# The last product of a three-stage attention/FFN kernel, written as seven quarter products

## The chip, the cores and the metric

One core of one Trainium2 chip runs the whole program. The metric is device time in microseconds (us) of one execution. Three runs of the kernel before took 1508.46, 1511.51 and 1515.61 us, a median of 1511.51. The engines are TensorE (PE in the rows; PEld is its weight load), VectorE (DVE), ScalarE (ACT), GpSimd (POOL) and SyncE (SP), whose queue issues the DMAs.

## What is computed

All inputs are float32 for the kernel except the six weight matrices, which arrive as float64 and are turned into float32 on the chip.

```python
kv = einsum('bhsd,bhse->bhde', k, v); out = einsum('bhsd,bhde->bhse', q, kv)   # 8 batches, 8 heads, 576 x 64
x = out / sqrt(mean(out*out, -1) + 1e-6) * g_norm                              # then 4608 tokens x 512
x = max(x @ w1, x @ w2, x @ w3) @ moe_w_out                                    # 512 -> 768 -> 512
g = s * relu(x @ w_in)**2 + b                                                  # 512 -> 2048
result = g @ w_out                                                             # 2048 -> 512
```

## The kernel before, in words

Tokens are kept in nine blocks of 512 columns with the features on the partitions: block b has the first 512 tokens of batch b, the ninth the last 64 tokens of all eight batches. Every float32 operand of a matmul is split into a high and a low part (`split`: a ScalarE copy, then a subtraction on VectorE or GpSimd), and each product is three matmuls (high x high, high x low, low x high).

Three stages follow one another on TensorE.

*Stage 1* does attention, norm and the first FFN, block by block, and writes the result to `x1d` in device memory. Beside it, w_in and w_out are read as float64 in 32 pieces (`p2_src`, `conv_load`), converted (`conv_unpack`, `conv_sum`) and stored to `wd`.

*Stage 2* is the w_in product by Strassen's scheme (Winograd's form). A set `q` of inputs is two blocks side by side; there are four wide sets (2 x 512 columns) and one narrow (2 x 256). `right` makes the seven inputs of a set, `left` the seven factors of each of four weight groups. For each set and group, `product` runs seven quarter products of 12 matmuls into PSUM tiles a, b and c, two each, some of them adding onto a tile that holds an earlier one. `combine` copies products 0, 1 and 2 out (ScalarE, the "cs" tiles), adds them to products 3, 4 and 5 (VectorE), squares (VectorE; GpSimd for product 6) and scales (`s*g+b`, ScalarE). `keep` stores the four quarters of the result in `gd`. That makes 20 groups of 7 x 12 matmuls.

*Stage 3* is the w_out product, tile by tile in the plain way: w_out is the moving operand (512 columns), a 128-token slice of g the stationary one. `g_load` reads g back, `g_split` splits it into one of six slots (tags h0 to h5), `gemm4` adds 16 x 3 matmuls for each of four token slices of a block into `acc`, `last_out` copies that out (ScalarE and VectorE in turn) and `store` writes 128 whole rows of the result, 2 KB each; for the ninth block two stores of 64 rows.

What sets the order: each step is put at a position of a plan by `at(pos, ...)` and sorted. On TensorE and SP the instructions stand in that order; on the other engines a scheduler orders them by a simulated time. A position in stages 2 and 3 is 12 matmuls; `T4` is where stage 3 starts. The steps that the change touches are planned in lines 705 to 731.

## Time and profile before

| | |
|---|---|
| median of three runs | 1511.51 us |
| the profiled execution, its own time | 1511.72 us |
| its span, first to last instruction | 1509.9 us |
| TensorE busy | 1437.8 us, 95% |
| VectorE, ScalarE, GpSimd busy | 744.6, 668.3, 415.5 us |
| DMA, mean over the span | 119 GB/s |

Busy time of an instruction runs from its start to its end; matmuls, and operations of VectorE and ScalarE, start before the one ahead has ended, so a rate is read from starts. "idle before <-X" in a row is the time for which the engine stood still ahead of it and the instruction whose end released it. A row of the profile that begins with L612 belongs to line 612 of the kernel.

### The profile page before, as it was taken

The page shows a single profiled execution, that of the slowest core. Times are in us where ns is not written, and L with a number is a line of the kernel's source. Part 1 is how long each engine was busy: PE and PEld are TensorE (multiplying, and loading weights), DVE is VectorE, ACT ScalarE, POOL GpSimd, SP SyncE. Part 2 cuts the span into 40 slices and gives each one's busy share as a digit, 9 for nine tenths or more (in the row PEclk, how much of TensorE's full clock was granted, in tenths as well). Part 3 has the DMA queues.
Part 4 walks back from the last instruction along what each step waited for, and adds up shares of the span by engine and source line. Part 5 has one row for each costly group of instructions (what it writes and reads, how often), then busy time and mean ns, then how long its engine had stood idle before and what let it go on. Part 6 is the DMA issues. An engine that isn't in the chain of part 4 may idle for free. (4 is left out here: it accounts for less than half of the span.)

```text
span 1509.9 us, 18507 instructions
## 1 busy us (share of the span) xinstructions
PE 1437.8 (95%) x6868; PEld 1173.1 (78%) x6868; DVE 744.6 (49%) x1129; ACT 668.3 (44%) x1153; POOL 415.5 (28%) x301
## 2 busy tenths in 40 slices
PE   4777899999999999999999999999999999999998
...
GB/s 206 198 190 87 63 73 103 90 125 102 126 87 140 87 139 22 112 8 112 77 105 158 136 112 175 95 163 129 192 251 137 77 86 120 139 140 140 139 84 28
DMA packets 173579, 179.48 MB, mean 119 GB/s; under 512 B 91440, under 2 KB 126256, under 8 KB 171824
## 3 DMA queue, kind: packets, MB, share of 16 engines
...
q14 instruction: 37, 0.30, 0.1%
...
## 5 line engine op out<-in xcount | busy, mean ns | idle before, releaser
L94 PE MATMUL g<-xh,w_w 128*128 128x512 f32 x648 | 258.3, 401 | 4.6 <-ACT xh L90 4.6
L95 PE MATMUL g<-xl,w_w 128*128 128x512 f32 x648 | 257.4, 397 | 0.0
L96 PE MATMUL g<-xh,w_w 128*128 128x512 f32 x648 | 256.9, 397 | 0.0
L680 PE MATMUL acc<-w_z,g 128*128 128x512 f32 x576 | 224.1, 389 | 0.0
L681 PE MATMUL acc<-w_z,g 128*128 128x512 f32 x576 | 224.1, 389 | 0.0
L682 PE MATMUL acc<-w_z,g 128*128 128x512 f32 x576 | 224.1, 389 | 0.0
L612 PE MATMUL ps_a<-x_q,w_q 128*128 128x512 f32 (+1 forms) x960 | 209.6, 369 | 7.2 <-ACT cs L621 5.6
L90 ACT ACTIVATE g<-gr 128x512 fp32r<-128x512 f32 x144 | 90.9, 631 | 267.7 <-PE acc L682 250.7
L91 DVE TENSOR_TENSOR g<-gr,g 128x512 fp32r<-128x512 f32 x108 | 75.6, 700 | 268.7 <-ACT g L90 267.4
L612 PEld LDWEIGHTS ps_a<-x_q,w_q 128*128 128x128 f32 x960 | 167.3, 188 | 41.2 <-ACT cs L621 8.4
L632 ACT ACTIVATE r<-r,sb_b,sb_s 128x512 f32<-128x512 f32 (+1 forms) x160 | 118.6, 766 | 82.1 <-DVE r L628 36.7
L94 PEld LDWEIGHTS g<-xh,w_w 128*128 128x128 f32 x648 | 123.4, 191 | 32.3 <-ACT xh L90 6.2
L95 PEld LDWEIGHTS g<-xl,w_w 128*128 128x128 f32 x648 | 124.2, 192 | 27.1 <-POOL tr_ctr L162 0.5
L96 PEld LDWEIGHTS g<-xh,w_w 128*128 128x128 f32 x648 | 123.9, 191 | 27.5 <-issue 0.5
L523 POOL TENSOR_TENSOR r<-r 128x512 f32<-128x512 f32 (+1 forms) x40 | 54.9, 1383 | 311.1 <-ACT r L630 309.8
L91 POOL TENSOR_TENSOR g<-gr,g 128x512 fp32r<-128x512 f32 x36 | 47.1, 1307 | 335.7 <-ACT g L90 335.7
L681 PEld LDWEIGHTS acc<-w_z,g 128*128 128x128 f32 x576 | 108.1, 188 | 22.5
L682 PEld LDWEIGHTS acc<-w_z,g 128*128 128x128 f32 x576 | 108.1, 188 | 22.4
L680 PEld LDWEIGHTS acc<-w_z,g 128*128 128x128 f32 x576 | 108.1, 188 | 22.3
L162 POOL TENSOR_TENSOR tr_ctr<-tr_ctr 128x512 int32<-128x512 int32 x42 | 55.5, 1320 | 197.9 <-ACT tr_ctr L155 181.4
L612 PE MATMUL ps_b<-x_q,w_q 128*128 128x512 f32 (+1 forms) x480 | 105.8, 369 | 0.8 <-ACT cs L621 0.7
L361 DVE TENSOR_TENSOR h<-g,h 128x512 f32<-128x512 f32 x108 | 74.0, 685 | 53.1 <-PE g L96 51.9
...
## 6 DMA issues: line engine op xcount, KB each, us to landing
gd<-r SPq DMA_DIRECT2D x128, 256.0 KB, 2.0
gr<-gd SPq DMA_DIRECT2D x64, 512.0 KB, 6.5
raw_craw<-in_moe_w_out_dram SPq DMA_DIRECT2D x20, 512.0 KB, 3.8
...
raw_craw<-in_moe_w_in_dram SPq DMA_DIRECT2D x16, 512.0 KB, 4.2
...
```

Of the source, the lines that this page charges most:

```text
L90: act(out=hi, in_=src, func=AF.Copy)
L91: eng.tensor_tensor(out=lo, in0=src, in1=hi.bitcast(F32), op=ALU.subtract)
L94: nc.tensor.matmul(ps, lhsT=w[:, 0, sl], rhs=xh, start=first, stop=False)
L95: nc.tensor.matmul(ps, lhsT=w[:, 0, sl], rhs=xl, start=False, stop=False)
L96: nc.tensor.matmul(ps, lhsT=w[:, 1, sl], rhs=xh, start=False, stop=last)
L162: nc.gpsimd.tensor_tensor(out=t, in0=t, in1=r, op=ALU.add)
L361: nc.vector.tensor_tensor(out=st["h", m], in0=ps, in1=st["h", m], op=ALU.max)
L612: nc.tensor.matmul(ps, lhsT=w[:, a, c], rhs=x[:, b_, :n], start=new and k == 0 and e == 0, stop=k == HK - 1 and e == 2, skip_group_check=True)
L632: act(out=h, in_=h, func=AF.Identity, scale=sb_s, bias=sb_b)
L680: mm(acc, lhsT=h[:, 0, sl], rhs=w[:, 0], start=(k == 0), stop=False)
L681: mm(acc, lhsT=h[:, 0, sl], rhs=w[:, 1], start=False, stop=False)
L682: mm(acc, lhsT=h[:, 1, sl], rhs=w[:, 0], start=False, stop=(k == M2 - 1))
```

## The change

Stage 3 now uses the seven quarter products too. The result is made feature-major. The 2048 inputs of w_out are cut in two parts, so each set has two *halves* H (10 in all, H even: first part, H odd: second), each with 7 products of 4 inputs x 2 output tiles x 3 matmuls, added up over the two parts in `xh`/`xl` tiles. The moving operand is now g (512 or 256 columns), the stationary one a factor of w_out.

Around that: `combine` keeps its result in the "cs" tile (a ring of 10, was 6), squares product 6 on ScalarE, gives products 3 and 6 the opposite sign, and adds two pairs on GpSimd, so that `gd` holds five quarters, with one sum of inputs made ready. `left` makes 28 factors of w_out during the last set of stage 2 (before: 16 splits), three of seven negated. w_out is loaded as float64 in four DMAs a piece, with columns in another order. After each odd half, `put` turns the result in squares of 32 x 32 on VectorE and stores it with four DMAs from 32 partitions each (512 B runs); for the narrow set, eight DMAs. The tiles of `put` are four: two tagged "t" and two "st".

```diff
+    neg = base.tile([P, 2], F32, name="neg")
-    gd = [dram.tile([P, 4, M2 // 2, N], F32, name=f"gd{q}") for q in range(B // 2 + 1)]
+    gd = [dram.tile([P, 5, M2 // 2, N], F32, name=f"gd{q}") for q in range(B // 2 + 1)]
...
     def p2_src(n):
-        n -= M2
-        return [(0, P, w2o[n * P:(n + 1) * P, :])]
+        r0 = i * DF2 // 2 + 2 * m * P
+        return [((2 * kk + b) * P, None,
+                 w2o[r0 + kk * P:r0 + (kk + 1) * P, :].rearrange("p (a b r) -> p b a r", a=4, b=4)[:, 2 * j + b])
+                for kk in range(2) for b in range(2)]
...
     def combine(G, q, g, i):
             if i < 3:
-                s_ = st["cs", i, m] = p2["pool"].tile([P, N], F32, tag="s", bufs=6, name=f"cs_{G}_{i}_{m}")
+                s_ = st["cs", i, m] = p2["pool"].tile([P, N], F32, tag="s", bufs=10, name=f"cs_{G}_{i}_{m}")[:, :n]
...
             if i < 6:
-                tt(nc.vector, h, ps, add, st["cs", {3: 2, 4: 1, 5: 0}[i], m][:, :n])
+                h = st["cs", 5 - i, m]
+                tt(nc.vector, h, ps, add, h)
+                stt(out=h, in0=h, scalar=0.0, in1=h, op0=ALU.max, op1=ALU.mult)
             else:
+                h = stage2(f"r_{G}_{m}")[:, :n]
                 act(out=h, in_=ps, func=AF.Relu)
-                tt(nc.gpsimd, h, h, ALU.mult, h)
-            act(out=h, in_=h, func=AF.Identity, scale=sb_s, bias=sb_b)
+                act(out=h, in_=h, func=AF.Square)
+            less = i in (3, 6)
+            act(out=h, in_=h, func=AF.Identity, scale=neg[:, 0:1] if less else sb_s, bias=neg[:, 1:2] if less else sb_b)
+            if i == 6:
+                d = st["r", 7, m] = stage2(f"d_{G}_{m}")[:, :n]
+                tt(nc.gpsimd, d, st["r", 4, m], add, h)
+                tt(nc.gpsimd, h, st["r", 5, m], add, h)
...
+    def z_right(H, i, k_):
+        n, z = width(H // 2), lambda i_: p2["z", i_, k_]
+        if i in (2, 3):
+            tt(nc.vector, z(1), z(1), add, z(0 if i == 2 else 5))
+        f = z(1 if 0 < i < 4 else i)
+        o = 28 * H + 4 * i + k_
+        x = hs["z", i, k_] = slot(HS[o % M1], f"zx_{o}")
+        split(x[:, 0, :n], x[:, 1, :n], f, nc.gpsimd if o % 6 == 5 else nc.vector)
+
+    def z_product(H, i, k_):
+        n, new = width(H // 2), i in (0, 1, 5)
+        kk = 4 * (H % 2) + k_
+        w, x = wt["q", 4 + kk // 2, i], hs["z", i, k_]
+        for m in range(2):
...
+            for e, (a, b_) in enumerate(((0, 0), (0, 1), (1, 0))):
+                nc.tensor.matmul(ps, lhsT=w[:, a, c], rhs=x[:, b_, :n], start=new and k_ == 0 and e == 0,
+                                 stop=k_ == 3 and e == 2, skip_group_check=True)
+
+    def z_combine(H, i):
...
+            if i < 3:
+                s_ = st["cs", i, m] = p2["pool"].tile([P, N], F32, tag="s", bufs=10, name=f"zc_{H}_{i}_{m}")[:, :n]
+                act(out=s_, in_=ps, func=AF.Copy)
+                if more:
+                    tt(nc.gpsimd, s_, s_, add, acc(5 - i, m))
+            elif i < 6:
+                tt(nc.vector, acc(i, m), ps, add, st["cs", 5 - i, m])
+            elif more:
+                tt(nc.vector, acc(i, m), ps, add, acc(i, m))
+            else:
+                act(out=acc(i, m), in_=ps, func=AF.Copy)
+
+    def put(H, c, u):
+        qq = H // 2
+        o = stage2(f"o_{H}_{c}_{u}").rearrange("p (b f) -> p b f", b=4)
+        for m in range(4):
+            nc.vector.transpose(o[:, :, 32 * m:32 * m + 32], p2["o"][c][:, m, u * P:(u + 1) * P])
+        for a in range(4):
+            f, part = slice(a * P, (a + 1) * P), slice(32 * a, 32 * a + 32)
+            if qq < NQ - 1:
+                r0 = (2 * qq + c) * S + u * P
+                nc.sync.dma_start(out=out[r0:r0 + P, f].rearrange("(b r) f -> r b f", r=32), in_=o[part])
+            else:
+                for e in range(2):
+                    r0 = (4 * c + 2 * u + e) * S + N
+                    nc.sync.dma_start(out=out[r0:r0 + REM, f].rearrange("(b r) f -> r b f", r=32),
+                                      in_=o[part, 2 * e:2 * e + 2])
...
+    for H in range(2 * NQ):
+        t = T4 + 14 * H
+        for i in range(7):
+            for kk in range(4):
+                at(t + 2 * i + 0.5 * kk - 2.4, z_right, H, i, kk)
+                at(t + 2 * i + 0.5 * kk, z_product, H, i, kk)
+            at(t + 2 * i + 1.9, z_combine, H, i)
...
+        if H % 2:
+            for c in range(2):
+                for u in range(width(H // 2) // P):
+                    at(t + 12.4 + 2 * c + 0.4 * u, put, H, c, u)
```

How the instructions stand. First ScalarE in stage 2, from the last product of group 13 on (the third wide set; no inputs are split here). In a name, the first number is the group, then product and output tile. Before (L621 copies, L630 is the relu of product 6, L632 the scaling):

```order
L630 ACTIVATE r_13_6_0_8236<-ps_a_13_0_8098 128x512
L632 ACTIVATE r_13_5_0_8214<-r_13_5_0_8214,sb_b_74,sb_s_73 128x512
L630 ACTIVATE r_13_6_1_8240<-ps_a_13_1_8099 128x512
L632 ACTIVATE r_13_5_1_8218<-r_13_5_1_8218,sb_b_74,sb_s_73 128x512
L632 ACTIVATE r_13_6_0_8236<-r_13_6_0_8236,sb_b_74,sb_s_73 128x512
L621 ACTIVATE cs_14_0_0_8260<-ps_a_14_0_8244 128x512
L632 ACTIVATE r_13_6_1_8240<-r_13_6_1_8240,sb_b_74,sb_s_73 128x512
L621 ACTIVATE cs_14_0_1_8262<-ps_a_14_1_8245 128x512
```

and in the change (L643 relu, L644 square, L646 scaling, L635 copies):

```order
L643 ACTIVATE r_13_0_8307<-ps_a_13_0_8173 128x512
L646 ACTIVATE cs_13_0_0_8189<-cs_13_0_0_8189,sb_b_74,sb_s_73 128x512
L643 ACTIVATE r_13_1_8314<-ps_a_13_1_8174 128x512
L644 ACTIVATE r_13_0_8307<-r_13_0_8307 128x512
L646 ACTIVATE cs_13_0_1_8191<-cs_13_0_1_8191,sb_b_74,sb_s_73 128x512
L644 ACTIVATE r_13_1_8314<-r_13_1_8314 128x512
L646 ACTIVATE r_13_0_8307<-r_13_0_8307,neg_75 128x512
L635 ACTIVATE cs_14_0_0_8337<-ps_a_14_0_8321 128x512
L635 ACTIVATE cs_14_0_1_8339<-ps_a_14_1_8322 128x512
L646 ACTIVATE r_13_1_8314<-r_13_1_8314,neg_75 128x512
L635 ACTIVATE cs_14_1_0_8355<-ps_b_14_0_8341 128x512
L635 ACTIVATE cs_14_1_1_8357<-ps_b_14_1_8342 128x512
```

Two squares have come in, and the scaling of product 6 no longer stands behind a GpSimd operation. GpSimd's four additions of group 13 need the scaled tiles r_13 and cs_13_0; the copies that come next (cs_14_2) go into the buffers of cs_13_0.

Second, ScalarE where stage 3 starts. Before, the last copies of stage 2 are followed by the first splits of g:

```order
L621 ACTIVATE cs_19_2_0_9128<-ps_a_19_0_9068 128x512
L621 ACTIVATE cs_19_2_1_9130<-ps_a_19_1_9069 128x512
L90 ACTIVATE g_0_0_9196<-gr_0_0_9102 128x512
L632 ACTIVATE r_19_3_0_9148<-r_19_3_0_9148,sb_b_74,sb_s_73 128x512
L632 ACTIVATE r_19_3_1_9152<-r_19_3_1_9152,sb_b_74,sb_s_73 128x512
L90 ACTIVATE g_0_1_9221<-gr_0_0_9102 128x512
```

In the change (zx_n is the n-th split input of stage 3, in the order in which TensorE needs them; zc a copy of a stage 3 product):

```order
L644 ACTIVATE r_19_1_9394<-r_19_1_9394 128x512
L646 ACTIVATE r_19_0_9387<-r_19_0_9387,neg_75 128x512
L91 ACTIVATE zx_5_9412<-z_0_1_9295 128x512
L646 ACTIVATE cs_19_0_0_9210<-cs_19_0_0_9210,sb_b_74,sb_s_73 128x512
L646 ACTIVATE r_19_1_9394<-r_19_1_9394,neg_75 128x512
L646 ACTIVATE cs_19_0_1_9212<-cs_19_0_1_9212,sb_b_74,sb_s_73 128x512
L705 ACTIVATE zc_0_0_0_9449<-zs_a_0_0_9401 128x512
L705 ACTIVATE zc_0_0_1_9451<-zs_a_0_1_9405 128x512
L91 ACTIVATE zx_8_9444<-z_0_0_9289 128x512
L91 ACTIVATE zx_6_9425<-z_0_2_9351 128x512
L91 ACTIVATE zx_9_9462<-z_0_1_9295 128x512
L91 ACTIVATE zx_7_9434<-z_0_3_9415 128x512
```

Inputs 6 and 7 of product 1 now stand behind the scalings of the last group and behind the copies of product 0.

Third, SP at the end, from its last load on. Before, the last stores of the narrow block (two each of 64 partitions); below it the change, with eight each of 32 partitions:

```order
L658 DMA gr_7_11511<-gd_96 128x2x256 x2
L671 DMA out_dram<-out_0_11622 64x512 x2
L671 DMA out_dram<-out_1_11638 64x512 x2
L671 DMA out_dram<-out_2_11654 64x512 x2
L671 DMA out_dram<-out_3_11670 64x512 x2
```

```order
L670 DMA z_6_1_12473<-gd_97 128x2x256
L729 DMA out_dram<-o_0_0_12781 32x2x128 x8
L729 DMA out_dram<-o_0_1_12800 32x2x128 x8
L729 DMA out_dram<-o_1_0_12827 32x2x128 x8
L729 DMA out_dram<-o_1_1_12840 32x2x128 x8
```

Eight issues have become 32.

## Rows read from the trace of the kernel before

**Rows 1.** The page, busy time: us, share of the span, instructions.

```profile
PE 1437.8 (95%) x6868; PEld 1173.1 (78%) x6868; DVE 744.6 (49%) x1129; ACT 668.3 (44%) x1153; POOL 415.5 (28%) x301
```

**Rows 2.** Busy time by stretch: PE, PEld, DVE, ACT, POOL; clock, DMA share, GB/s.

```profile
0.00:755.50 755.50, 696.02 (x3460) 556.78 (x3461) 445.56 (x643) 335.29 (x589) 313.62 (x225) 0.97 0.40 107
755.50:1113.40 357.90, 349.90 (x1681) 292.11 (x1680) 211.04 (x363) 231.74 (x403) 53.65 (x40) 1.00 0.42 151
1113.40:1505.10 391.70, 391.70 (x1729) 324.24 (x1727) 87.95 (x125) 100.71 (x162) 48.28 (x37) 1.00 0.30 112
```

**Rows 3.** Timeline of PE in stage 2: start, length, instructions; wide, then narrow.

```profile
1091.65 5.60 PE L612 MATMUL ps_a<-x_q,w_q 128*128 128x512 f32 x24
1097.09 2.88 PE L612 MATMUL ps_b<-x_q,w_q 128*128 128x512 f32 x12
...
925.61 1.60 PE L612 MATMUL ps_a<-x_q,w_q 128*128 128x256 f32 x12
927.05 1.60 PE L612 MATMUL ps_b<-x_q,w_q 128*128 128x256 f32 x12
```

**Rows 4.** Waits of PEld in stage 2: us in total, times, longest.

```profile
PEld ps_a L612 <- ACT cs L621: 8.4, 7, 2.8
```

**Rows 5.** Timeline of stage 2 where a new set's inputs are split.

```profile
1030.31 0.69 DVE L523 TENSOR_TENSOR r<-ps_a,cs 128x512 f32<-128x512 f32 x1
1030.91 0.68 DVE L91 TENSOR_TENSOR x_q<-t,x_q 128x512 fp32r<-128x512 f32 x1
...
1036.08 5.23 POOL L523 TENSOR_TENSOR r<-r 128x512 f32<-128x512 f32 x2 [17.30 <-ACT r L630]
...
1040.35 0.81 ACT L632 ACTIVATE r<-r,sb_b,sb_s 128x512 f32<-128x512 f32 x1 [2.63 <-POOL r L523]
```

**Rows 6.** Timeline of POOL in stage 2: another such place, and a quiet group.

```profile
834.28 5.56 POOL L523 TENSOR_TENSOR r<-r 128x512 f32<-128x512 f32 x2 [17.19 <-ACT r L630]
855.25 2.23 POOL L523 TENSOR_TENSOR r<-r 128x512 f32<-128x512 f32 x2 [15.41 <-ACT r L630]
```

**Rows 7.** Groups by line and shape: count, busy us, mean ns, idle before.

```profile
L523 POOL TENSOR_TENSOR r<-r 128x512 f32<-128x512 f32 x32 | 44.9, 1414 | 273.5 <-ACT r L630 272.5
L267 DVE STREAM_TRANSPOSE qt<-qraw 128x576 f32<-128x576 f32 x32 | 24.5, 770 | 26.1 <-PE orps L289 16.6 <-DMA qraw<-in_q_dram 8.1 <-PE kvps L232 1.4
L523 DVE TENSOR_TENSOR r<-ps_a,cs 128x256 f32<-128x256 f32 x8 | 3.2, 423 | 0.0
```

**Rows 8.** Timeline of ACT in stage 2: four splits, three scalings, back to back.

```profile
1050.30 2.20 ACT L90 ACTIVATE w_z<-wor 128x512 fp32r<-128x512 f32 x4 [4.11 <-DMA wor<-wd]
...
1042.02 2.21 ACT L632 ACTIVATE r<-r,sb_b,sb_s 128x512 f32<-128x512 f32 x3
```

**Rows 9.** Timeline of the end: last matmul, last copy, last two stores.

```profile
1504.86 0.39 PE L682 MATMUL acc<-w_z,g 128*128 128x512 f32 x1
1505.29 0.60 ACT L687 ACTIVATE out<-acc 128x512 f32<-128x512 f32 x1 [4.84 <-PE acc L682]
1505.91 1.11 SPq L671 DMA_DIRECT2D out_dram<-out  x2
```

**Rows 10.** SP's issues by line, ns min/median/max; landing of L671's stores.

```profile
L667 SPq DMA_DIRECT2D out_dram<-out x32: 332/335/351, 1155.8 to 1462.4; - x32
...
L671 SPq DMA_DIRECT2D out_dram<-out x8: 466/508/766, 1497.8 to 1506.4; - x8
DMA to landing us min/median/max: 2.2/2.3/2.5
...
L263 SPq DMA_DIRECT2D qraw<-in_q_dram x16: 465/528/1842, 3.2 to 22.1; - x16
```

**Rows 11.** DMA issues (KB, us to landing); VectorE's wait for w_out, 360 to 640 us.

```profile
raw_craw<-in_moe_w_out_dram SPq DMA_DIRECT2D x20, 512.0 KB, 3.8
...
qraw<-in_q_dram SPq DMA_DIRECT2D x28, 288.0 KB, 4.5
...
DVE gc_cgc L152 <- DMA raw_craw<-in_moe_w_out_dram: 42.4, 11, 11.2
```

More of the change, by code (lines that the diff above doesn't have):

```diff
@@ L512, in tmp, with stage2 @@
     def tmp(nm):
-        return p2["pool"].tile([P, N], F32, tag="tmp", bufs=4, name=nm)
-    nstage = [0]
-    def ctile(nm):
-        nstage[0] += 1
-        pool, tag, bufs = [(p2["pool"], "c", 4), (base, "t", 2), (p2["pool"], "c", 4), (base, "st", 2)][nstage[0] % 4]
-        return pool.tile([P, N], F32, tag=tag, bufs=bufs, name=nm)
+        return p2["pool"].tile([P, N], F32, tag="c", bufs=4, name=nm)
+    turn = [0]
+    def stage2(nm):
+        turn[0] += 1
+        return base.tile([P, N], F32, tag=("t", "st")[turn[0] % 2], bufs=2, name=nm)
     def tt(eng, out, in0, op, in1):
@@ L554, in left @@
             make(2, s_[1], sub, a11)
-        elif i == 6:
             make(4, a12, sub, s_[2])
         f = {0: a11, 3: a22, 5: a12}.get(i)
-        w = wt["q", g, i] = slot(WS[g][i], f"w_q_{g}_{i}")
-        split(w[:, 0], w[:, 1], s_[{1: 3, 2: 2, 4: 1, 6: 4}[i]] if f is None else f, nc.vector)
+        f = s_[{1: 3, 2: 2, 4: 1, 6: 4}[i]] if f is None else f
+        w = wt["q", g, i] = slot(WS[g % 4][i], f"w_q_{g}_{i}")
+        if g < 4 or i not in (3, 4, 5):
+            split(w[:, 0], w[:, 1], f, nc.vector)
+        else:
+            act(out=w[:, 0], in_=f, func=AF.Copy, scale=-1.0)
+            stt(out=w[:, 1], in0=f, scalar=-1.0, in1=w[:, 0].bitcast(F32), op0=ALU.mult, op1=sub)
     def width(q):
@@ L645, in wo_split @@
-    def wo_split(k):
-        w = wt["z", k] = slot((WS[0] + WS[1] + WS[2])[k], f"w_z_{k}")
-        split(w[:, 0], w[:, 1], p2["wo", k // 4][:, k % 4], nc.vector)
-    def g_load(j, u):
-        r = p2["g", u] = slot(f"l{u}", f"gr_{j}_{u}", F32)
-        q, c, n = j // 2, j % 2, width(j // 2)
-        i, m = divmod(u, M2 // 4)
-        m = slice(2 * m, 2 * m + 2)
-        if j < B:
-            nc.sync.dma_start(out=r, in_=gd[q][:, 2 * i + c, m])
-        else:
-            for c in range(2):
-                nc.sync.dma_start(out=r[:, :, c * n:(c + 1) * n], in_=gd[q][:, 2 * i + c, m, :n])
@@ L660, in g_split @@
-    def g_split(j, k):
-        h = hs[j, k] = slot(HS[(j * M2 + k) % M1], f"g_{j}_{k}")
-        split(h[:, 0], h[:, 1], p2["g", k // 2][:, k % 2], nc.vector if k % 4 else nc.gpsimd)
-    def store(j, t, o):
-        if j < B:
-            r0 = j * S + t * P
-            nc.sync.dma_start(out=out[r0:r0 + P, :], in_=o)
-        else:
-            for i in range(P // REM):
-                r0 = (t * (P // REM) + i) * S + N
-                nc.sync.dma_start(out=out[r0:r0 + REM, :], in_=o[i * REM:(i + 1) * REM])
@@ L673, in gemm4 @@
[L673 to L690 removed]
+            nc.sync.dma_start(out=gd[q][:, {5: 0, 4: 1, 3: 2, 7: 3, 6: 4}[i], 2 * g + m, :width(q)], in_=st["r", i, m])
@@ new lines, in attention_max_ffn_relu2_ffn, with z_load @@
+    KEPT = {0: 0, 6: 1, 5: 2, 4: 4}
+    GS = {0: ("l0", "l1"), 4: ("l6", "l7"), 6: ("l2", "l3"), 5: ("l4", "l5")}
+    def z_load(H, i, u):
+        q, n = H // 2, width(H // 2)
+        k0 = 4 * (H % 2)
+        if i == 1:
+            t = p2["z", 1, u] = tmp(f"z_{H}_{u}")[:, :n]
+            nc.sync.dma_start(out=t, in_=gd[q][:, 3, k0 + u, :n])
+            return
+        t = slot(GS[i][u], f"z_{H}_{i}_{u}", F32)
+        nc.sync.dma_start(out=t[:, :, :n], in_=gd[q][:, KEPT[i], k0 + 2 * u:k0 + 2 * u + 2, :n])
+        for e in range(2):
+            p2["z", i, 2 * u + e] = t[:, e, :n]
@@ new lines, in z_combine @@
+    def z_combine(H, i):
+        n, more = width(H // 2), H % 2
+        if i == 0 and not more:
+            p2["o"] = [base.tile([P, KD, N], F32, tag=tg, name=f"{tg}o_{H}") for tg in ("xh", "xl")]
+        acc = lambda i_, m: p2["o"][i_ in (4, 6)][:, 2 * (i_ in (3, 4)) + m, :n]
+        for m in range(2):
+            ps = st["ps", BANK[i], m][:, :n]
+            if i < 3:
+                s_ = st["cs", i, m] = p2["pool"].tile([P, N], F32, tag="s", bufs=10, name=f"zc_{H}_{i}_{m}")[:, :n]
+                act(out=s_, in_=ps, func=AF.Copy)
+                if more:
[6 more added lines that the diff above has]
+                act(out=acc(i, m), in_=ps, func=AF.Copy)
@@ L712, in attention_max_ffn_relu2_ffn @@
                 if i > 2:
-                    at(pos + 2.4, keep, qq, g, i)
+                    at(pos + 2.4 + (i == 6), keep, qq, g, i)
+            at(pos + 3.2, keep, qq, g, 7)
         if n:
```

65 lines of the change are left out of this document (22 added, 43 removed).

## The prediction, before the changed kernel had run

> **What bounds the kernel now.** I read the page's busy shares first: TensorE is busy 95% of the span [rows 1]. A share over the span says nothing of single stages, so I cut the trace at the first product of w_in and the first product of w_out (busy time by stretch) [rows 2]. Three stages come out: 755.5 us for attention and the first FFN, 357.9 us for the w_in product (stage 2), 391.70 us for the w_out product (stage 3). In stage 3 TensorE is busy for all of the 391.70 us at full clock, VectorE for 88 and ScalarE for 101. So stage 3 is as long as its matmuls, and a matmul less is time off the span.
>
> What a matmul costs is read from starts, since durations overlap. Between 1091.65 and 1097.09 there are 24 matmuls of 512 columns: 5.44 / 24 = 0.2267 us each [rows 3]. Stage 3 has 9 tiles x 16 x 4 x 3 = 1728 of them, 1728 x 0.2267 = 391.7 us, the whole stage. Of 256 columns, 12 matmuls take 927.05 - 925.61 = 1.44 us, 0.120 each [rows 3]. Stage 2 would take 1344 x 0.2267 + 336 x 0.120 = 345.0 us by this; it takes 357.9, so 12.9 us are waits, mostly for ScalarE's copies out of PSUM [rows 4]. At the end, 1509.9 - 1505.1 = 4.8 us lie behind the last matmul (its start plus 0.23): a copy, two store issues, their landing [rows 9].
>
> **The change part by part.** The sum is made against the profiled execution, 1511.7 us (span 1509.9 and 1.8 around it); the median of the runs is 1511.5, the same within 0.2.
>
> *Fewer matmuls.* Each half has 7 products x 4 x 2 x 3 = 168 matmuls. Eight halves are 512 wide (1344), two are 256 wide (336): 304.7 + 40.3 = 345.0 us in place of 391.7. **-46.7 us**, all on the path.
>
> *Hand-over from stage 2.* Before, stage 3 starts without a gap [rows 2]. Now ScalarE's queue holds, around the last w_in product, the squares and scalings of that group, the last of 28 splits of w_out's factors, and the first input splits. From the timeline a split comes out every 0.52 us, a scaling every 0.70 [rows 8]; VectorE starts an operation every 0.60 [rows 5]. Input 0 needs a slot that is free at -5.4 us (counted from the last w_in matmul). From there to the first row of the change's ScalarE rows above lie 8 splits, 4 scalings and 3 other operations of about 0.5: 8.5 us, and 0.2 of waiting for the last product, so that row starts at 3.3. Going on, the copy for input 5 ends at 5.0, for input 6 at 9.1, for input 7 at 10.2, the latter two behind a PSUM copy that can't start before product 0 is done (5.4). VectorE's subtraction makes input 6 ready at 9.8; it is needed at 8.5. Five operations stand between on VectorE: input 7 is ready at 12.8, needed at 11.2. Input 5 (GpSimd) is some 0.3 late. 0.3 + 1.3 + 1.6 = **+3.2 us**; 0 if ScalarE arrives early, 8 if GpSimd is late as well.
>
> *Steady halves.* A split input feeds 6 matmuls (1.36 us). For two wide halves (76.2 us of matmuls) VectorE has 47 splits, 16 additions and 14 accumulations at 0.60 and 32 turns. A turn of 576 columns takes 0.770 [rows 7], one operation of 512 lasts 0.69 and starts 0.60 after the one before [rows 5], one of 256 lasts 0.423 [rows 7]; by that slope a turn of 128 is some 0.29 long, 0.20 apart. Together 53 us of 76: hidden. The stores hide too: 32 issues at 0.555 are 18 us of SP's 76. Where it is tight is behind an odd half: 32 turns beside the next half's splits, and the four tiles of the second side each wait for four stores of the first (2.2 us of issue a tile, 2.3 landing). Walking the queue there, the third product's inputs are ready about when they are needed; with GpSimd in between I take 1 us for each of three places. **+3 us**, 0 to 18.
>
> *Narrow halves.* A split input feeds 0.72 us of matmuls there, while the stores of the wide half before still take 16 x 0.555 = 8.9 us and hold the turns, with splits queued behind them. **+4.5 us**, 0 to 12.
>
> *The end.* Before, two stores were left behind the last matmul. Now 32 are: the first side is turned some 0.3 us before the last matmul ends (the product before ends 24 x 0.120 = 2.9 us earlier; two additions and six turns follow). A store of 128 partitions takes SP 0.335, one of 64 partitions 0.508 median (1.11 for two with the gap), a load into 32 partitions 0.528 [rows 9, 10]. A store from 32 partitions isn't shown; nearest are the 64-partition stores of the same tensor and the 32-partition loads, so 0.555. 32 x 0.555 = 17.8, landing 2.3 [rows 10]: -0.3 + 17.8 + 2.3 = 19.8 us behind the last matmul in place of 4.8. **+15.0 us**; +9.2 at 0.375, +21.9 at 0.77.
>
> *Stage 2.* ScalarE gets two squares more for each group (of 19.0 us), GpSimd four additions for two products. The wait of ScalarE's scaling for GpSimd goes (2.63 us at 1040.35, with TensorE's copies queued behind it) [rows 5]. Next in line is the ring of ten "cs" tiles: the third pair of copies of a group reuses tiles that GpSimd adds into last. In the order shown above the squares and scalings end at 5.8 us behind the group's last product; the four additions, 1.115 each in a quiet stretch [rows 6], end at 8.6, the copy is due at 8.7, and TensorE waits from 10.9 on: 1.7 us to spare. Quiet groups lose nothing. Where a new set of inputs is split, two additions took 5.2 to 5.6 [rows 5, 6]; four lose some 3 us at three or four such places, and the wait that goes gives about 6 back. The last set has 28 splits and 16 additions in place of 16 splits; ScalarE then has some 16 of 19 us. **+4 us**, -6 to +35.
>
> *Stage 1.* A load of w_out is four DMAs with runs of 256 B in place of one with 4 KB: three more issues of SP, 1.0 to 1.6 us by [rows 10], for each of 16. q's loads have runs of 128 B and land in 4.5 us against 3.8 [rows 11]. VectorE's waits for these loads of up to 11.2 us [rows 11] are idle time beside matmuls. **+1 us**, 0 to 6.
>
> Sum: -46.7 + 3.2 + 3 + 4.5 + 15.0 + 4 + 1 = -16.0, so 1511.7 - 16.0 = **1496 us**.
>
> *A rule beside the rows.* Two GpSimd operations last 2.23 us in a quiet stretch and 5.23 where VectorE starts one every 0.60 [rows 5, 6]: they are held up, not slowed a little. The Trainium skill (SBUF — State Buffer, section "SBUF: two separate sides") calls the port pair that GpSimd shares with VectorE an exclusive lock, which a VectorE operation with two SBUF inputs takes as well; the trace agrees. By it the 63 two-input operations of a wide pair exclude GpSimd's 15: 63 x 0.60 + 15 x 1.115 = 54.5 us of 76, so the sum for stage 3 would stay; it speaks against the change in stage 2, as the second rival.
>
> **The rivals.**
> - *Cheap stores and a lighter stage 2* (17%). A 32-partition store costs what a 128-partition one does (the row of the first tiles' stores is for it, the 64-partition rows are against), the turns fit, and stage 2 gains 5 from the wait that goes: -46.7 + 9.2 + 3.2 - 5 = -39.3, 1472 us; half of that 1484.
> - *The ring of "cs" tiles* (10%), the one that ends slower. Its place is ScalarE's third pair of copies in each of 20 groups, its price what four additions take above 4.46 + 1.7 us. If GpSimd's addition means 2.0 us, each group loses 3.5 - 1.7 = 1.8: 36 us in place of 4, 1528. It decides from a mean of 1.9 on. For it: 32 operations had a mean of 1.414 [rows 7], and VectorE's load grows in the last set. Against: most pairs took 2.23.
> - *Turns and stores hold VectorE* (12%). At 0.77 a store, the last tile of a side comes free 3.4 us later, and GpSimd's operations cost VectorE three times 1 us: 6 at each of three places, 9 in the narrow halves, 27 in place of 7.5: 1516.
> - *The saving isn't had* (6%): six slots hold the split inputs, so a split must come within 5 x 1.36 = 6.8 us of its slot's release. If ScalarE's and VectorE's queues take 0.1 us too much for each of 280 inputs, 28 us go, less 7.5 counted above: 1516. Against: alone, the two steps need 0.52 + 0.69.
> - My forecast keeps 55%, from 1484 to 1508.
>
> **How the numbers follow.** About 0.5% (7.6 us) is what a measurement of this kernel can tell from no change. Faster (under 1503.9): forecast 53, cheap stores 17, the third and fourth rival 3, together 73%. Same: 2 + 8 + 5 + 2 = 17%. Slower: 8 from the ring, 2 from the turns, 10%. Range 1480 to 1514: it leaves out the best of the first rival and the ring's upper part.
>
> **What would show it.** Last matmul's end about 31 us earlier than before, and some 20 us behind it with SP issuing stores back to back. Stage 3 from first to last matmul near 356. At its start TensorE waits for ScalarE or VectorE in the second product, 2 to 5 us. Stage 2 within 355 to 370; TensorE's waits there still name ScalarE's copies. I am wrong in mechanism if stage 3 is over 365, if stage 2 grows past 375, or if less than 12 us lie behind the last matmul.

## The result, and the profile after

The changed kernel took 1492.35 us (median of four runs, 1489.72 to 1495.04), the kernel before 1512.21 (four runs beside them, 1508.46 to 1515.61). The ratio is 0.987, 95% interval 0.984 to 0.990: faster by 1.3%. The prediction was 1496, with a range of 1480 to 1514 and 73% on faster. The profiled execution is the quickest of the four, 1489.72 us with a span of 1487.8; of before it was 1511.7 and 1509.9. So the traces are 22.1 us apart, 6.1 more than the sum of the prediction.

The page's busy time, for [rows 1]:

```profile
PE 1397.1 (94%) x6820; PEld 1143.4 (77%) x6820; DVE 985.7 (66%) x1561; ACT 784.2 (53%) x1393; POOL 524.9 (35%) x381
```

TensorE works 40.7 us less, VectorE 241 us more, ScalarE 116 and GpSimd 109. Where the time went shows in the same cuts as [rows 2], at the first product of w_in, the first of w_out, and the last matmul's end (busy time by stretch: PE, PEld, DVE, ACT, POOL; then clock, DMA share, GB/s):

```profile
0.00:754.35 754.35, 697.00 (x3461) 556.74 (x3462) 447.61 (x645) 334.48 (x589) 312.50 (x225) 0.97 0.48 108
754.35:1116.39 362.04, 350.16 (x1681) 292.51 (x1680) 239.20 (x388) 251.74 (x450) 102.31 (x76) 1.00 0.46 167
1116.39:1471.45 355.06, 349.85 (x1681) 294.12 (x1679) 297.53 (x526) 197.95 (x356) 110.12 (x80) 0.99 0.52 157
1471.45:1487.80 16.35, 0.10 (x1) 0.00 (x0) 1.36 (x6) 0.00 (x0) 0.00 (x0) 0.60 0.25 64
```

Stage 1 is 1.15 us shorter than before, stage 2 is 4.1 longer, stage 3 is 36.64 shorter, and 16.35 us lie behind the last matmul where 4.8 lay [rows 9], 11.55 more: -1.15 + 4.14 - 36.64 + 11.55 = -22.1, the difference of the spans.

**Stage 3.** Its matmuls alone are 345.0 us, so 10.1 are lost. The timeline of PE has most of it in the second and third product (a wide product is 5.44 us from start to start when nothing waits):

```profile
1116.39 5.60 PE L693 MATMUL zs_a<-zx,w_q 128*128 128x512 f32 x24
1121.83 1.75 PE L693 MATMUL zs_b<-zx,w_q 128*128 128x512 f32 x7
1124.16 1.65 PE L693 MATMUL zs_b<-zx,w_q 128*128 128x512 f32 x6 [0.58 <-POOL zx L92]
1129.31 2.38 PE L693 MATMUL zs_b<-zx,w_q 128*128 128x512 f32 x6 [3.50 <-DVE zx L92]
1132.32 2.50 PE L693 MATMUL zs_b<-zx,w_q 128*128 128x512 f32 x5 [0.63 <-DVE zx L92]
1134.62 6.66 PE L693 MATMUL zs_a<-zx,w_q 128*128 128x512 f32 x24
1141.11 5.60 PE L693 MATMUL zs_b<-zx,w_q 128*128 128x512 f32 x24
```

From 1121.83 to 1141.11 are 19.28 us in place of 10.88: 8.40 lost, of which 4.71 are waits and the other 3.69 slower matmuls. The last five matmuls of the second product last 2.3 us where five take 1.13. The stretches name the reason, in the column after the busy times, TensorE's granted clock:

```profile
1116.39:1130.30 13.91, 9.83 (x42) 7.48 (x41) 11.49 (x14) 9.94 (x18) 8.02 (x5) 0.99 0.94 364
1130.30:1134.80 4.50, 3.87 (x10) 2.58 (x9) 4.37 (x8) 1.75 (x3) 0.00 (x0) 0.50 0.39 117
1134.80:1137.00 2.20, 2.20 (x7) 1.68 (x6) 0.69 (x1) 1.63 (x3) 0.43 (x1) 0.55 0.81 237
```

Behind the wait of 3.50 us the clock falls to 0.50, 1.2 GHz in place of 2.4, and stays there until shortly before 1137. The timelines of POOL, DVE and ACT show what TensorE waited for:

```profile
1120.61 2.27 POOL L530 TENSOR_TENSOR d<-cs,r 128x512 f32<-128x512 f32 x1 [13.29 <-ACT r L646]
1122.84 1.27 POOL L92 TENSOR_TENSOR zx<-z,zx 128x512 fp32r<-128x512 f32 x1
1124.08 1.28 POOL L530 TENSOR_TENSOR r<-cs,r 128x512 f32<-128x512 f32 x1
1125.32 1.72 POOL L530 TENSOR_TENSOR d<-cs,r 128x512 f32<-128x512 f32 x1
1127.12 1.59 POOL L530 TENSOR_TENSOR r<-cs,r 128x512 f32<-128x512 f32 x1
```

```profile
1121.04 0.69 DVE L530 TENSOR_TENSOR z<-z,z 128x512 f32<-128x512 f32 x1
1124.15 1.77 DVE L530 TENSOR_TENSOR z<-z,z 128x512 f32<-128x512 f32 x1 [2.42 <-POOL zx L92]
1125.84 3.42 DVE L92 TENSOR_TENSOR zx<-z,zx 128x512 fp32r<-128x512 f32 x2
1129.18 0.68 DVE L530 TENSOR_TENSOR z<-z,z 128x512 f32<-128x512 f32 x1
...
1131.59 1.88 DVE L92 TENSOR_TENSOR zx<-z,zx 128x512 fp32r<-128x512 f32 x3
```

```profile
1124.02 1.16 ACT L91 ACTIVATE zx<-z 128x512 fp32r<-128x512 f32 x2
```

GpSimd's split stands behind an addition of stage 2's last group. VectorE's next operation overwrites the tile that this split reads, so it stands still for 2.42 us. Then three VectorE operations take 5 us beside three additions on GpSimd, and 0.60 each once GpSimd is done (1129.18). The second of the two subtractions at 1125.84 is that of input 6: ScalarE's copy for it ended at 1125.18, but it ends at 1129.26 only, and TensorE goes on at 1129.31.

The other places that the prediction feared lose little. Behind the wide puts no product lasts longer than 5.44. The fourth products of halves 1 and 7, which don't stand behind a put, last 5.92 and 5.96, with waits of 0.19 and 0.18 us for VectorE's splits; in the narrow halves one product lasts 3.48 in place of 2.88.

**Stage 2.** The waits of PE and its loads, for [rows 4] (total, times, longest), name VectorE's additions where ScalarE's copies stood:

```profile
PEld ps_a L625 <- DVE cs L530: 11.7, 9, 2.3
PE ps_a L625 <- DVE cs L530: 8.4, 8, 1.9
```

**The end.** The last product starts at 1468.51, SP issues 32 stores back to back, and they land in 1.6 us:

```profile
1470.57 14.90 SPq L729 DMA_DIRECT2D out_dram<-o  x32
```

14.90 / 32 = 0.466 us from issue to issue, where the prediction took 0.555 from the 64-partition stores (1.11 for two, [rows 9]).

### The profile page after: what moved, and what is told of

The parts are those of the page before. It is cut to its first block, busy times and chain, and to the rows that moved or that the text cites. A ratio compares the mean times of both kernels' runs of the same rounds, so it can differ in the third digit from the quotient of the medians.

```text
span 1487.8 us, 19756 instructions
## 1 busy us (share of the span) xinstructions
PE 1397.1 (94%) x6820; PEld 1143.4 (77%) x6820; DVE 985.7 (66%) x1561; ACT 784.2 (53%) x1393; POOL 524.9 (35%) x381
## 4 chain that ended last, share of the span: by engine, by line
PE 36%; DVE 6%; issue 5%; DMA 4%; ACT 2%; POOL 2%; SPq 0%; DVEq 0%; POOLq 0%; ACTq 0%
PE zs_a L693 12%; PE ps_a L625 6%; PE zs_b L693 6%; PE zs_c L693 3%; PE ps_b L625 3%; PE g L96 1%; PE g L97 1%; PE g L95 1%; PE ps_c L625 1%; DVE cs L530 1%; DMA xl<-x1d 1%; DMA z<-gd 1%; DVE zx L92 1%; POOL d L530 1%; DVE x_q L92 1%
## 5 line engine op out<-in xcount | busy, mean ns | idle before, releaser
L91 ACT ACTIVATE zx<-z 128x512 fp32r<-128x512 f32 (+1 forms) x280 | 162.0, 588 | 148.8 <-PE zs_a L693 56.3
L693 PE MATMUL zs_a<-zx,w_q 128*128 128x512 f32 (+1 forms) x960 | 203.2, 369 | 0.0
L625 PEld LDWEIGHTS ps_a<-x_q,w_q 128*128 128x128 f32 x960 | 167.4, 188 | 46.0 <-DVE cs L530 11.7
L92 DVE TENSOR_TENSOR zx<-z,zx 128x512 fp32r<-128x512 f32 (+1 forms) x234 | 172.2, 754 | 36.4 <-ACT zx L91 35.9
L693 PEld LDWEIGHTS zs_a<-zx,w_q 128*128 128x128 f32 x960 | 168.7, 189 | 30.4
L530 POOL TENSOR_TENSOR d<-cs,r 128x512 f32<-128x512 f32 (+1 forms) x40 | 59.8, 1503 | 282.7 <-ACT r L646 227.3
L92 POOL TENSOR_TENSOR zx<-z,zx 128x512 fp32r<-128x512 f32 (+1 forms) x46 | 60.0, 1303 | 210.8 <-ACT zx L91 210.8
L693 PE MATMUL zs_b<-zx,w_q 128*128 128x512 f32 (+1 forms) x480 | 105.6, 374 | 5.2 <-DVE zx L92 4.5
L693 PEld LDWEIGHTS zs_b<-zx,w_q 128*128 128x128 f32 x480 | 84.6, 191 | 23.0 <-DVE zx L92 6.8
L625 PEld LDWEIGHTS ps_b<-x_q,w_q 128*128 128x128 f32 x480 | 84.2, 188 | 16.1 <-ACT cs L635 1.0
L96 PE MATMUL g<-h,w_o 128*128 128x512 f32 x216 | 85.6, 396 | 10.1 <-DVE h L92 10.1
L95 PE MATMUL g<-h,w_o 128*128 128x512 f32 x216 | 86.5, 400 | 6.3 <-ACT w_o L91 4.2
```

Source lines behind the costliest of these rows:

```text
L91: act(out=hi, in_=src, func=AF.Copy)
L92: eng.tensor_tensor(out=lo, in0=src, in1=hi.bitcast(F32), op=ALU.subtract)
L95: nc.tensor.matmul(ps, lhsT=w[:, 0, sl], rhs=xh, start=first, stop=False)
L96: nc.tensor.matmul(ps, lhsT=w[:, 0, sl], rhs=xl, start=False, stop=False)
L530: eng.tensor_tensor(out=out, in0=in0, in1=in1, op=op)
L625: nc.tensor.matmul(ps, lhsT=w[:, a, c], rhs=x[:, b_, :n], start=new and k == 0 and e == 0, stop=k == HK - 1 and e == 2, skip_group_check=True)
```

## The experiments

Each edit is made to the changed kernel. "Stage 2" is from the first product of w_in to the first of w_out, "stage 3" from there to the end of the last matmul, "hand-over" the second and third product of w_out (10.88 us if nothing waits, 19.28 in the changed kernel).

**1. Half of the last stores on ScalarE's queue.**

```diff
-                    nc.sync.dma_start(out=out[r0:r0 + REM, f]...
+                    (nc.scalar if a % 2 else nc.sync).dma_start(out=out[r0:r0 + REM, f]...
```

> Half of the 32 last stores is issued by ScalarE's queue, the other half by SyncE's. In the changed kernel 16.35 us lie behind the last matmul, 14.90 of them 32 issues of 0.466. Theory (the issue of stores sets the end): two queues of 16 take some 7.5 us, so about 9 us lie behind the last matmul and the span falls by 7 us. Rival (the transfers themselves or the turns set the end): 15 to 16.5 us stay, the span changes by less than 1 us. Second rival (ScalarE's queue issues at twice SyncE's price): about 13 us stay.

1486.2 us (1483.54 to 1490.99), ratio to before 0.9825 [0.980, 0.985]. The timelines of the two queues:

```profile
1473.30 7.49 SPq L729 DMA_DIRECT2D out_dram<-o  x16
```

```profile
1473.31 7.59 ACTq L729 DMA_DIRECT2D out_dram<-o  x16
```

The last product starts at 1471.24, so with 2.88 for it 9.1 us lie behind the last matmul in place of 16.35. The end was issue time: two queues issue side by side at the old price each. The Trainium skill (Perfetto Trace Analysis, section "DMA Optimizations") says that balancing DMAs over several engines may help where descriptor generation is the bottleneck; the trace agrees in so far as 14.90 us of issues became 7.49 and 7.59 side by side.

**2. Every store in two halves.**

```diff
-                nc.sync.dma_start(out=out[r0:r0 + P, f].rearrange("(b r) f -> r b f", r=32), in_=o[part])
+                for x in range(2):
+                    nc.sync.dma_start(out=out[r0 + 64 * x:r0 + 64 * x + 64, f].rearrange("(b r) f -> r b f", r=32),
+                                      in_=o[part, 2 * x:2 * x + 2])
```

> Every store of the output is cut in two of half the size: 64 issues at the end in place of 32, and 64 in place of 32 behind each of the four wide pairs. Theory (an issue costs the same whatever its size, and the end is issues): 16.35 us behind the last matmul become 31, and the wide pairs stay hidden, since 64 x 0.47 = 30 us of SyncE stand against 76 us of matmuls; stage 3 from first to last matmul grows by less than 4 us. Rival (issue goes by bytes): the end stays at 16 to 17 us. Second rival (my prediction's price for puts, tiles that wait for their stores): stage 3 grows by 10 us or more.

1525.5 us (one run). Behind the last matmul lie 31 us, as expected (the narrow stores are cut alike; 64 issues in 29.84, 0.466 each): an issue of 16 KB costs what one of 32 KB did. Stage 3 grew to 367.4, 12.3 more, against the expectation that it stays hidden. SP from its last wide stores on, and PE in the last narrow half:

```profile
1434.98 31.15 SPq L726 DMA_DIRECT2D out_dram<-o  x64
1466.22 0.90 SPq L670 DMA_DIRECT2D z<-gd  x2
```

```profile
1469.60 5.74 PE L693 MATMUL zs_a<-zx,w_q 128*128 128x256 f32 x24 [11.92 <-ACT zx L91]
```

The wide stores stand in SP's queue ahead of the loads that the last narrow half needs. A narrow half has 7 x 2.88 = 20.2 us; 32 issues (16.7 us in the changed kernel, from 1428.03) fit in it, 64 don't. So what can go wrong there isn't turns on VectorE but loads behind stores on SP. The wait of 11.92 us is again followed by half clock (the product takes 5.5 in place of 2.88).

**3. One split of the first half moved to VectorE.**

```diff
-        split(..., f, nc.gpsimd if o % 6 == 5 else nc.vector)
+        split(..., f, nc.gpsimd if o % 6 == 5 and o != 5 else nc.vector)
```

> The one input split of the first half that GpSimd makes in front of the second product (the sixth) goes to VectorE. In the changed kernel the second w_out product takes 12.79 us in place of 5.44, the third 6.49. Theory (VectorE stands 2.42 us behind GpSimd's split, which stands behind an addition of stage 2): that wait goes, one VectorE operation of 0.6 comes, so the two products take 16 to 17.5 in place of 19.28. Rival (the additions on GpSimd slow VectorE's two-input operations, and this is all of it): under 1 us is won.

1495.39 us (one run). The hand-over takes 18.04, 1.24 less, but that is no gain that this run can show: with the same code there it took 17.19 to 19.71 in the profiled executions of the changed kernel and of runs 1, 2, 8 and 9, as the clock fell earlier or later. TensorE's waits are the firmer sign, and they stay: 4.66 us (0.71, 1.51, 2.44) in place of 4.71, with half clock behind them. VectorE's wait for the tile is gone, but its operations beside GpSimd's additions still take up to 1.77 us. So the theory fails, and the rival stands.

Here a second thing shows. Stage 2, untouched by the edit, took 365.80 us in place of 362.04, and the waits at its set boundaries are the same. The timeline of PE at one of them, in the changed kernel and in this run:

```profile
830.16 0.97 PE L625 MATMUL ps_a<-x_q,w_q 128*128 128x512 f32 x3 [1.11 <-DVE cs L530]
831.96 4.40 PE L625 MATMUL ps_a<-x_q,w_q 128*128 128x512 f32 x18 [0.83 <-DVE cs L530]
```

```profile
832.80 0.98 PE L625 MATMUL ps_a<-x_q,w_q 128*128 128x512 f32 x3 [1.11 <-DVE cs L530]
834.60 6.69 PE L625 MATMUL ps_a<-x_q,w_q 128*128 128x512 f32 x21 [0.82 <-DVE cs L530]
```

The same two waits; then 18 matmuls in 4.40 us there, 21 in 6.69 here (21 x 0.2267 = 4.76). The same stretch of this run by microseconds, with the granted clock third from the end:

```profile
835.00:836.00 1.00, 1.00 (x5) 0.81 (x4) 1.00 (x3) 0.34 (x1) 0.00 (x0) 0.68 0.34 135
836.00:837.00 1.00, 1.00 (x4) 0.81 (x3) 1.00 (x3) 0.31 (x2) 0.00 (x0) 0.50 0.33 127
```

The clock fell behind these waits here and not there. It fell at three boundaries of this run, at none in the changed kernel's profiled one: 3.8 us between two runs of the same stage. Over the six profiled runs whose stage 2 is the changed kernel's it takes 362.0 to 365.8 us, with falls at none to three boundaries.

**4. That split, and the last group's four additions, on VectorE.**

```diff
+                eng = nc.vector if G == 4 * NQ - 1 else nc.gpsimd
-                tt(nc.gpsimd, d, st["r", 4, m], add, h)
-                tt(nc.gpsimd, h, st["r", 5, m], add, h)
+                tt(eng, d, st["r", 4, m], add, h)
+                tt(eng, h, st["r", 5, m], add, h)
```

(and run 3's edit)

> As the run with one split moved, and the four additions of the last group of stage 2 also go from GpSimd to VectorE. Theory (what is left of the hand-over is GpSimd's additions shutting VectorE out): five more VectorE operations of 0.60 = 3.0 us, but none of 1.7; the second and third product take 12 to 14 us in place of 19.28, stage 3 is 5 to 7 us shorter. Rival (VectorE's queue is full there whoever adds): 16 us or more, no better than the one split alone.

1489.24 us (1485.23 to 1491.74), ratio to before 0.985 [0.982, 0.987]. The hand-over takes 14.47, 0.5 above the expected band, and stage 3 is 350.3, 4.8 shorter. VectorE has five operations more in its queue and TensorE waits less. PE there:

```profile
1126.90 1.66 PE L694 MATMUL zs_b<-zx,w_q 128*128 128x512 f32 x6 [0.86 <-DVE zx L92]
1129.91 1.43 PE L694 MATMUL zs_b<-zx,w_q 128*128 128x512 f32 x5 [1.35 <-DVE zx L92]
1131.17 5.60 PE L694 MATMUL zs_a<-zx,w_q 128*128 128x512 f32 x24
```

No wait exceeds 1.35 us (a third, of 0.52, is for ScalarE) and the next product has its 5.44 again: the clock stays up. So most of the hand-over's 8.4 us was GpSimd's additions and the half clock behind them; 3.6 remain.

**5. GpSimd's additions of stage 2 left out.**

```diff
-                d = st["r", 7, m] = stage2(f"d_{G}_{m}")[:, :n]
-                tt(nc.gpsimd, d, st["r", 4, m], add, h)
-                tt(nc.gpsimd, h, st["r", 5, m], add, h)
+                st["r", 7, m] = st["r", 4, m]
```

> GpSimd's four additions for each group of stage 2 are left out: two of the five kept planes are then stored without their addition, so the output isn't the reference's. The changed kernel's stage 2 took 362.04 us in its profiled run, with 8.4 us of TensorE's waits on VectorE's additions in eight places. Theory (GpSimd's additions shut VectorE's two-input operations out, so VectorE is late for the last product of a group where a new set is split): these waits fall to under 3 us, stage 2 takes 352 to 358 us, and the hand-over (the second and third w_out product, 19.28 us) falls to 15 or less. Rival (ScalarE's added squares and VectorE's own queue at a new set make it late): 7 us or more of waits stay, stage 2 is 360 or more.

1475.06 us (one run). Stage 2 takes 351.9 and the hand-over 14.1; the waits of PE for VectorE:

```profile
PE ps_a L625 <- DVE cs L530: 1.8, 3, 0.8
```

8.4 us of waits for VectorE become 1.8 (those for ScalarE go from 3.3 to 1.6). The additions cost stage 2 10.1 us (362.04 - 351.9), though no instruction of TensorE waits for one. And without them stage 2 is 6.0 shorter than before the change (357.9).

**6. The additions of every group on VectorE.**

```diff
-                tt(nc.gpsimd, d, st["r", 4, m], add, h)
-                tt(nc.gpsimd, h, st["r", 5, m], add, h)
+                tt(nc.vector, d, st["r", 4, m], add, h)
+                tt(nc.vector, h, st["r", 5, m], add, h)
```

> The same four additions of every group go from GpSimd to VectorE. Theory (what costs is that the two engines shut each other out, not the work): 76 operations of 0.60 on VectorE and none at 1.2 to 4 on GpSimd beside it; stage 2 is 355 to 361 us, hand-over 12 to 15 us in place of 19.28, the time 5 to 10 us below the changed kernel's 1492. Rival (VectorE's queue is what binds at a new set): stage 2 is 364 or more and TensorE's waits on VectorE exceed 8.4.

1478.76 us (1478.21 to 1479.67), ratio to before 0.978 [0.976, 0.980]; stage 2 354.5, hand-over 15.2. The time is 13.6 below the changed kernel's median, more than expected. VectorE has 80 additions more, and TensorE's waits in the stage still fall, to 1.7 us for VectorE and 2.6 for ScalarE. The same place of the program in the changed kernel (POOL, then DVE) and in this run (DVE):

```profile
1022.69 1.75 POOL L530 TENSOR_TENSOR d<-cs,r 128x512 f32<-128x512 f32 x1
1024.52 1.62 POOL L530 TENSOR_TENSOR r<-cs,r 128x512 f32<-128x512 f32 x1
```

```profile
1023.20 1.78 DVE L92 TENSOR_TENSOR x_q<-t,x_q 128x512 fp32r<-128x512 f32 x1
1025.02 1.67 DVE L530 TENSOR_TENSOR t<-xh,t 128x512 f32<-128x512 f32 x1
1026.61 1.28 DVE L92 TENSOR_TENSOR x_q<-t,x_q 128x512 fp32r<-128x512 f32 x2
```

```profile
1021.03 1.29 DVE L92 TENSOR_TENSOR x_q<-t,x_q 128x512 fp32r<-128x512 f32 x2
1022.24 0.69 DVE L530 TENSOR_TENSOR t<-xh,t 128x512 f32<-128x512 f32 x1
```

Beside GpSimd two VectorE operations hold the queue from 1023.20 to 1026.61, 3.4 us in place of 1.2. VectorE is then 2.2 us late for product 4's addition, and the group's last product waits 1.11 and 0.84 us for it at 1033.96. In this run that product starts without a wait. The four runs lie within 1.5 us, the changed kernel's within 5.3: no fall of the clock shows in the stage. This run keeps the early split on GpSimd and run 4 has it on VectorE: 15.2 against 14.5 for the hand-over, so the split is worth some 0.7 us once the additions are gone.

**7. The squares back on GpSimd.**

```diff
-                act(out=h, in_=h, func=AF.Square)
+                tt(nc.gpsimd, h, h, ALU.mult, h)
```

> The squares of each group's last product go back from ScalarE to GpSimd, where they stood before the change. Theory of my prediction (the wait of ScalarE's scaling for GpSimd, with TensorE's copies queued behind it, cost about 6 us, which the change took away, and two more operations on GpSimd lock VectorE out for longer): stage 2 grows by 4 us or more over the changed kernel's 362 to 366. Rival (that wait was idle time beside matmuls): within 2 us.

1508.52 us (one run); stage 2 takes 375.7, 13.7 more than in the changed kernel's profiled run and 10 more than in the longest of runs 1 to 9 with its stage 2, as the theory has it. ScalarE's scaling waits 10.8 us for GpSimd (not at all in the changed kernel). TensorE's waits grow from 11.7 to 16.8 us: from 3.3 to 7.3 for ScalarE's copies, from 8.4 to 9.5 for VectorE's additions. The rest is matmuls that last longer, mostly at half clock, which this execution has at four places of the stage. Stage 2 of this run, where the changed kernel's has 350.16 us of PE busy for the same matmuls and a clock of 1.00:

```profile
757.20:1132.91 375.71, 358.81 (x1681) 296.09 (x1680) 249.67 (x388) 237.97 (x414) 147.09 (x114) 0.98 0.45 165
```

By this one run, moving the squares to ScalarE was worth 10 to 14 us once GpSimd also adds; without it the change would have gained almost nothing.

**8. w_out loaded as before.**

```diff
-        r0 = i * DF2 // 2 + 2 * m * P
-        return [((2 * kk + b) * P, None,
...
+        n -= M2
+        return [(0, P, w2o[n * P:(n + 1) * P, :])]
```

> w_out is loaded in stage 1 as before the change, one transfer for each of 16 parts in place of four; its rows and columns then stand in another order, so the output isn't the reference's. Theory (three more issues of 0.33 to 0.62 us for each part are hidden): stage 1 is 753 to 759 us, as in the changed kernel's runs (754.35 to 759.63), VectorE's longest wait for such a load is back at about 11 us. Rival (the smaller transfers gain or cost something): stage 1 leaves that band.

1490.46 us (one run); stage 1 is 754.61 us, VectorE's longest wait for a load 11.4. The four smaller loads cost nothing that can be seen.

**9. Stores of 128 partitions.**

```diff
-                nc.sync.dma_start(out=out[r0:r0 + P, f].rearrange("(b r) f -> r b f", r=32), in_=o[part])
+                r1 = r0 + 32 * a
+                nc.sync.dma_start(out=out[r1:r1 + 32, :].rearrange("r (a f) -> a r f", a=4), in_=o[:, a])
```

(and the same for the narrow ones, 16 in place of 32)

> Each store takes 32 rows of the output from all 128 partitions in place of a quarter of the features from 32 partitions: 16 stores at the end in place of 32, all on SyncE's queue. Theory (the end is issues, and the earlier 128-partition stores took SyncE 0.335 us each): 16 x 0.335 = 5.4 us in place of 14.9, so 7 to 8.5 us lie behind the last matmul in place of 16.35. Rival (a DMA that splits its side into three dimensions issues as slowly as the 32-partition stores, 0.466): 16 x 0.466 = 7.5, 9 to 9.5 us. Second rival (512 pieces of 512 B for each store move slower than they are issued): 11 us or more.

1497.12 us (one run). The theory falls, and so does its first rival. SP's issues of the last wide pair, and at the end:

```profile
1430.20 22.48 SPq L725 DMA_DIRECT2D out_dram<-o  x32
...
1479.61 10.93 SPq L731 DMA_DIRECT2D out_dram<-o  x16
```

10.93 / 16 = 0.683 us, 22.48 / 32 = 0.70, against 0.466 and 16.71 / 32 = 0.52 for the 32-partition stores. The second rival holds: the transfers are slower than their issues. Here is the stretch behind SP's last issue, which ends at 1490.54 (DMA share and GB/s are the last two numbers), and below it a stretch of run 1 with two queues of 32-partition stores:

```profile
1490.50:1492.00 1.50, 0.00 (x0) 0.00 (x0) 0.00 (x0) 0.00 (x0) 0.00 (x0) 0.50 0.29 86
```

```profile
1477.00:1480.90 3.90, 0.00 (x0) 0.00 (x0) 0.00 (x0) 0.00 (x0) 0.00 (x0) 0.61 0.54 137
```

The DMA moves 76 to 87 GB/s from 1481 on and goes on for 3 us behind the last issue; 16 stores of 64 KB at 86 GB/s are 12.2 us. The end is 14.7 us, 1.6 less; the last narrow half lost more, since 22.5 us of stores don't fit in 20.2 (PE waits 3.59 us for its inputs, half clock behind it).

**10. and 11. All findings together, with these stores; and without GpSimd's splits.**

> All three findings at once: stage 2's additions on VectorE, the one split in front of the second w_out product on VectorE, stores from 128 partitions with half of the last ones on ScalarE's queue. By the sum of the single runs: additions -13.6 against the changed kernel's 1492.35, end -10 to -12 (3 to 5 us of issues and landing on two queues), split -0.5 to -1: 1466 to 1469 us. Rival (the gains overlap, since the clock drops that the additions take away are counted twice, or the end is bound by turns and landing): 1470 to 1474.

> As the combined kernel, and all 45 other input splits of the w_out product go from GpSimd to VectorE too. Theory (what is left in stage 3 is VectorE's queue at the hand-over, and elsewhere GpSimd's splits hide): stage 3 from first to last matmul stays within 1 us of the combined kernel's, the time within 0.2%. Rival (GpSimd's splits still cost VectorE time where it counts): 1 to 3 us shorter. Second rival (VectorE is short of time behind the puts): longer by 2 us or more.

1483.46 us (1482.76 to 1484.74) and 1482.41 (1482.01 to 1483.12): both worse than run 6 alone. Stage 2 is 354.6 and 354.4 as in run 6, but stage 3 is 357.3 and 356.1 against run 6's 350.9, mostly by the wait in the last narrow half (3.58 and 2.23 us, then half clock). The end takes 14.8 and 14.9 us: on two queues eight such stores took SP 8.24 and ScalarE 10.09 us, over 1 us each, while the DMA moved the same 86 GB/s at a share of 0.29 as with one queue in run 9. So for these stores the transfers set the end, and a second queue can't shorten it. GpSimd's 45 other splits make no difference that these two runs can tell: 1.2 us in stage 3, with the loads' wait in both.

**12. The same, with the 32-partition stores.** Runs 1, 3 and 6 in one kernel.

> The combined kernel with the stores of the changed kernel (32 partitions, half of the last 32 on ScalarE's queue) in place of the 128-partition ones. Theory (the combined kernel lost to the run with the additions on VectorE only by its stores: 3.58 us of waiting and a half-clock stretch in the last narrow half, and 0.68 to 1.26 us an issue): stage 3 is back at 350 us or less, 9 us lie behind the last matmul, 1478.76 - 7.4 for the end - 0.7 for the split = 1470 to 1472 us. Rival (something else in the combination costs): 1475 or more.

1471.17 us (1470.12 to 1476.74), ratio to before 0.974 [0.972, 0.976]: the best of all, 2.6% under before, 1.4% under the changed kernel. Stage 3 and the end:

```profile
1115.59:1465.80 350.21, 346.98 (x1681) 292.37 (x1679) 296.75 (x531) 198.03 (x356) 102.56 (x75) 1.00 0.52 159
1465.80:1474.90 9.10, 0.16 (x2) 0.00 (x0) 1.42 (x6) 0.00 (x0) 0.00 (x0) 0.72 0.45 115
```

Both are as expected. The profiled execution is the slowest of the five, and the excess is in stage 1, which no edit touched: 760.4 us, where the changed kernel's had 754.35.

## Why the prediction was right, and where it was off

The forecast's mechanism held in the main: 1496 was said, 1492.35 came, and the case was the one given 55%. Term by term, against the profiled execution:

- **Matmuls, -46.7.** Right. Undisturbed products lasted 5.44 and 2.88 us, as [rows 3] give.
- **Hand-over, +3.2, measured 8.4** (6.3 to 8.8 over the five profiled executions with the same code there). The term that was undersized most, in three of the five past its own bound of 8. The late GpSimd split itself came out near what was said (0.58 us of wait against 0.3). Two steps failed. The first is "VectorE's subtraction makes input 6 ready at 9.8". ScalarE's copy for it was in time (done at 8.8 where 9.1 was said, counted, as there, from the last w_in matmul's end, 1116.39), but VectorE was not: it had stood 2.42 us for the tile that GpSimd's split still read, and three of its operations then took 5.0 us beside GpSimd's additions in place of 1.8. Input 6 was ready at 12.9. The five operations behind it ran at 0.60 each, as counted. Run 4, which takes the split and the additions off GpSimd, brings the hand-over to within 3.6 us of its matmuls; run 3 shows that the split alone isn't the cause. The second step is that nothing was counted for the clock behind a wait: 3.69 of the 8.4 are slower matmuls.
- **Steady halves, +3, measured 1.0; narrow halves, +4.5, measured 0.6.** Both oversized, and the 1.0 is not behind the puts, where the prediction had it, but in the fourth products of two halves. Stores, turns and splits did share VectorE and SP without harm. Run 2 shows what would bind there: SP's stores ahead of the next half's loads, not turns waiting for stores as the third rival had it.
- **The end, +15.0, measured 11.5.** The mechanism is right (runs 1 and 2), two sizes were off: 0.466 us an issue in place of 0.555, landing 1.6 in place of 2.3. The price lay between the bounds 0.375 and 0.77, below the nearest rows.
- **Stage 2, +4, measured +4.1.** Run 5 splits it as the prediction did: without the additions the stage is 6.0 shorter than before ("the wait that goes gives about 6 back"), and the additions cost 10.1 ("some 3 us at three or four such places"). That the sum fits to 0.1 is luck: over the six profiled executions with this stage 2 it is +4.1 to +7.9, as the clock falls at none to three boundaries. And the 6.0 is all that the change did to stage 2 beside the additions, not that wait alone; the wait itself is seen in run 7. The step that failed is the path: the prediction let TensorE wait for ScalarE's copies, through the ring of cs tiles; it waits 8.4 us for VectorE's additions and 3.3 for the copies, since VectorE is what GpSimd holds up. So the waits that "what would show it" named for this stage were the wrong ones. The ring didn't decide: GpSimd's wide additions lasted 1.5 us on average, under the 1.9 of the second rival.
- **Stage 1, +1, measured -1.15.** No effect (run 8); the profiled runs of this stage lie between 754.35 and 760.37 whatever the edit.

Part of the nearness is luck. Stage 3 took 355.06 us where the terms give 391.7 - 46.7 + 3.2 + 3 + 4.5 = 355.7, because 5.2 too little in the hand-over met 5.9 too much in the halves. In the whole sum the oversized terms (steady and narrow halves, end, stage 1: 11.5 us) and the undersized hand-over (5.2) leave 6.3 less, against 6.1 in the spans; the rest is 0.1 in stage 2 and rounding. The median lies 2.6 above the profiled run: the two longer executions (1494.49 and 1495.04) had a mean granted clock of 0.975 and 0.976, the two shorter ones 0.978 and 0.980.

The rule of the shared port pair carried further than the prediction took it. By the Trainium skill (SBUF — State Buffer, section "SBUF: two separate sides") GpSimd and a VectorE operation with two SBUF inputs exclude each other; it was weighed here by what VectorE does to GpSimd. The runs show the other direction to be the dear one: the VectorE operation of 0.60 us became 1.7 (run 6's rows). The additions that take one input from PSUM kept their length, which agrees with the rule too: the twelve wide ones of the changed kernel's stages 2 and 3 that ran mostly beside a GpSimd operation had a mean of 683 ns, the others 686.
